# First weight unit behind the third load of x, later ones one load later; last weight loads every second step; ScalarE sends the last tile's first half

## The chip, the cores and the metric

One core of a Trainium2 chip. TensorE multiplies, VectorE, ScalarE and GpSimd work element by element, and SyncE (SP) issues most of the transfers. The metric is the device time of one execution in microseconds (us), the median of several timed executions.

## The reference

Two layers of gated products stand behind a Fourier transform of x along the sequence and along the features, of which the real part is kept:

```python
X = np.fft.fft(x, axis=1)              # x: (2, 3008, 256)
x = np.fft.fft(X, axis=2).real.reshape(6016, 256)
gate = 1 / (1 + np.exp(-(x @ w_gate))) # w_gate, w_val: (256, 1536)
x = gate * (x @ w_val) @ w_out         # w_out: (1536, 256)
h = x @ w_in                           # w_in: (256, 2048)
return (h * np.cos(h)) @ w_out2        # (2048, 256)
```

## The kernel before

The sequence transform of length 3008 is split into 47 times 64. The first part, of length 47, runs over 16 **chunks** of 8 feature pairs (L487); a **load of x** (`load_x2`) brings two chunks and is issued as three transfers of 32 partitions each (`rows`, L430). There are eight loads and three buffers, `raw` 0 to 2, so a load waits until TensorE has read the buffer's chunks of three loads earlier. PSUM holds three chunks; each is copied to SBUF (`evac`, L500 and L503) by VectorE or ScalarE. The first load comes in pieces of its own (L439, L440). Chunk 6 also needs a small extra tensor, `x0`. Then the second transform, of length 64 (L543, L544), and the third, over features (L583), follow.

Weights arrive as 64-bit patterns and are decoded on the chip in **units** of 512 KB by a chain of steps over ScalarE (L177, L152, L158, L190), VectorE (L153, L160, L164, L169) and GpSimd (L174, L238, L239, L193). `u_0_64` to `u_0_75` are the twelve units of the first layer's gate and value weights (`w1`), `u_0_76` to `u_0_80` and one more those of its output weights (`wo1`), and a small row unit (24 KB, in `eo_82` at first) comes ahead of all. The sixteen units of the second layer (`w2`) are decoded during the gating steps, written to DRAM (`ws`, L223) and read again later (`w2_load`, L715).

The 72 **gating steps** (`step1`) each take three-matmul products (L641 to L643), VectorE's L659 and L667, ScalarE's sigmoid (L853) and two casts, GpSimd's L671 and an accumulating transfer (L710), and four steps later the output products (L684 to L687). The last 192 steps make the second layer (L641 to L643 for the hidden values, L759 to L775 for the cosine, L739 for the output); each tile of results leaves by L743 and, for the last half, L753.

The order of instructions on each engine is written by a **planner** in the program itself: it keeps a clock for each engine (`clk`), gives each step of a unit a cost, and fills what it takes for idle time (`fill`, `slot`) up to a due time. The order is fixed when the program is built. At run time each engine works through its list and waits on semaphores. SP's queue is one such list: a transfer that has to wait holds back all that are listed behind it.

Of the kernel before, what the change touches and what calls it, by code (L numbers as in the profile page):

```python
# [40 lines left out]
L1, L2 = 4, 5  # L41
# [14 lines left out]
def fft_moe_moe(ctx: ExitStack, tc: tile.TileContext, x, x0, head, w1, w1s, wo1, w2, t1, t3, out):  # L56
# [9 lines left out]
    nc = tc.nc  # L66
    V, A, G, PE = nc.vector, nc.scalar, nc.gpsimd, nc.tensor
# [33 lines left out]
    def WO2(f):  # L101
        return slots[8 + f // 2][:, f % 2 * UC:(f % 2 + 1) * UC].rearrange("p (h m) -> p h m", h=2)
# [13 lines left out]
    sas = flat1[:, GV0 + 8 * TW:GV0 + 9 * TW].rearrange("p (g c) -> p g c", g=2)  # L116
# [9 lines left out]
    DQ = nc.sync  # L126
    clk = {V: 0.0, A: 0.0, G: 0.0, DQ: 0.0}
# [133 lines left out]
    def cost(step, e):  # L261
        return (step[1][e] if step[0] in (VG, VA) else step[1]) + (beside[0] if e is V else 0)

    def may(un, e):

        step = un[2][0]
        if step[0] not in (VG, VA):
            return e is step[0]
        if e not in step[0] or begun[0] and step[0] is VG and e is V:
            return False  # L270
        if begun[0] and step[0] is VG:
            return True
        other = step[0][1 - step[0].index(e)]
        mine, theirs = (max(un[3], clk[q]) + step[1][q] for q in (e, other))
        return mine <= theirs + (VLATE if e is V else 0)

    def room_at(at, forced=False):

        fits = [bf for bf in free if max(at, bf[2]) + LIFE <= bf[1] and (forced or bf[2] <= at + .3)]
        return min(fits, key=lambda bf: (bf[1], bf[2])) if fits else None  # L280

    def step_of(un, e=None):
        if len(un[2][0]) > 3 and not un[1]:
            at = max(un[3], clk[un[2][0][0]])
            while not (room_at(at, True) or free):
                finish(next(o for o in live if o[1] and o[0][0] in DIRECT))
            bf = room_at(at) or room_at(at, True) or free[0]
            free.remove(bf)
            un[1].append(bf)
            un[4].append(bf[0])  # L290
            un[3] = max(un[3], bf[2])
        step = un[2].pop(0)
        if step[0] in (VG, VA):
            e = e or (G if begun[0] and step[0] is VG else min(step[0], key=lambda q: max(clk[q], un[3]) + step[1][q]))
            step[2](e)
        else:
            e = step[0]
            step[2]()
        un[3] = spend(e, cost(step, e), un[3]) + ((5.0 if begun[0] else 3.3) if e is DQ else .15)
        if not un[2]:  # L300
            live.remove(un)
            free.extend([buf, end, un[3], of] for buf, end, _, of in un[1])

    def load_next():
        k = queued.pop(0)
        load(*k, slots[home(*k)])
        loaded[k] = spend(DQ, 1.5) + 2.8

    def pairs():

        found = [[bf for bf in free if bf[3] == of] for of in STAGES]
        return [pair for pair in found if len(pair) == 2]

    def start(bfs):
        for bf in bfs:
            free.remove(bf)
        k = todo.pop(0)
        room = [stages[STAGES.index(bfs[0][3])] if len(bfs) == 2 else bf[0] for bf in bfs[:1]]
        live.append([k, bfs, unit_steps(*k, room), max([loaded.get(k, 0.0)] + [bf[2] for bf in bfs]), room])

    def begin(until):

        while todo and todo[0] in loaded and loaded[todo[0]] <= until:
            start([])

    def fill(e, until):

        while True:
            begin(until)
            for un in live:  # L330
                step = un[2][0]
                if may(un, e):
                    at = max(un[3], clk[e])
                    if len(step) > 3 and not un[1] and not room_at(at):
                        continue
                    if at + cost(step, e) <= until:
                        step_of(un, e)
                        break
            else:
                if e is DQ and clk[e] + 1.5 <= until:  # L340
                    if queued:
                        load_next()
                        continue
                    if len(todo) > held[0] and todo[0][0] == "w2":
                        ready = [p for p in pairs() if max(bf[2] for bf in p) <= until]
                        if ready:
                            start(ready[0])
                            continue
                return
# [72 lines left out]
    with tc.tile_pool(name="xp", bufs=1) as xp:  # L422
# [9 lines left out]
        def load_x2(p):  # L432

            raw, src = raws[p % NX2].rearrange("p (c j) s n -> p c j s n", c=2), x[:, 2 * p:2 * p + 2]
            rows(DQ, raw, src)
            spend(DQ, 2.2)
# [19 lines left out]
        clk[DQ] = 4.3  # L456
        for p in range(1, NX2):
            load_x2(p)
            if p == 1:
                fill(DQ, clk[DQ] + 1.7)  # L460
        DQ.dma_start(out=xs[0:96], in_=x0)


        for _ in range(NWARM):
# [249 lines left out]
    def w2_load(u, q):  # L714
        q.dma_start(out=f32(slot_tile(u, F32R)), in_=ws[u])  # L715
# [5 lines left out]
    def hid(s):  # L721
        tt, f = divmod(s, NF2)
        y = ys[tt]
        o = ps[:, 4 + s % 4, 0:PC]
        for k in range(2):
            three(o, W2(f)[:, k, 0], W2(f)[:, k, 1], y[:, 0, k], y[:, 1, k], first=(k == 0), last=(k == 1))

    def out2(s):
        tt, f = divmod(s, NF2)
        h = h2.pop(s)  # L730
        last = s == N2S - 1


        order = [(0, 0, 0), (0, 1, 0), (1, 0, 0), (1, 1, 0), (0, 0, 1), (1, 0, 1)]
        if last:
            order = order[:2] + order[4:5]
        for d, i, m in order:
            o = ps[:, 2 * (tt % 2) + d, 0:PC]
            PE.matmul(o, WO2(f)[:, i, d * 128:(d + 1) * 128], h[:, m],  # L739
                      start=(f == 0 and i == m == 0), stop=(m == 1 and (f == NF2 - 1 or d == 1 and s == N2S - 2)))  # L740
            if m == 1 and f == NF2 - 1:
                A.mul(sas[:, d], o, 2.0)
                nc.sync.dma_start(out=out[tt, d], in_=sas[:, d])  # L743
            if m == d == 1 and s == N2S - 2:
                V.tensor_scalar(out=sas[:, 1], in0=o, scalar1=2.0, scalar2=None, op0=ALU.mult)
        if last:
            for k, c0 in enumerate((0, PC - 256)):
                o, new = ps[:, 4 + k, 0:256], slice(256 * k - c0 * k, 256)
                for i, m in ((0, 0), (1, 0), (0, 1)):
                    PE.matmul(o, WO2(f)[:, i, 128:], h[:, m, c0:c0 + 256], start=(i == m == 0), stop=(m == 1))  # L750
                y = sas[:, 1, 256 * k:256 + (PC - 256) * k]
                V.scalar_tensor_tensor(out=y, in0=o[:, new], scalar=2.0, in1=y, op0=ALU.mult, op1=ALU.add)
                nc.sync.dma_start(out=out[tt, 1, :, 256 * k:256 + (PC - 256) * k], in_=y)  # L753

    def cos_a(s):
        h = ps[:, 4 + s % 4, 0:PC]
        k = ks[s % 2].bitcast(I32)
        r = rt[s] = rs[s % 3]
        A.activation(out=k, in_=h, func=AF.Copy, scale=INV2PI)  # L759
        V.scalar_tensor_tensor(out=r, in0=k, scalar=-C1, in1=h, op0=ALU.mult, op1=ALU.add)  # L760
        V.scalar_tensor_tensor(out=r, in0=k, scalar=-C2, in1=r, op0=ALU.mult, op1=ALU.add)  # L761

    def cos_b(s):
        r = rt[s]
        A.activation(out=r, in_=r, func=AF.Abs)  # L765
        A.activation(out=r, in_=r, func=AF.Sin, scale=-1.0, bias=HALFPI)  # L766
        V.tensor_tensor(out=r, in0=r, in1=ps[:, 4 + s % 4, 0:PC], op=ALU.mult)  # L767

    def cos_c(s):
        r = rt.pop(s)  # L770
        if s % 2 == 0:
            pair[0] = ghs[s // 2 % 3]
        h = h2[s] = pair[0][:, s % 2]
        A.copy(h[:, 0], r)  # L774
        (V if s == N2S - 1 else G).tensor_tensor(out=h[:, 1], in0=r, in1=f32(h[:, 0]), op=ALU.subtract)  # L775
# [124 lines left out]
    late = list(range(NF1 - 1, 16))  # L900
    for s in range(L1, N2S + L2):
        if s < N2S:
            hid(s)
            cos_a(s)
        if s >= L2:
            out2(s - L2)
        if s - 1 < N2S:
            cos_b(s - 1)
        if s - 2 < N2S:
            cos_c(s - 2)  # L910
        if late:
            u = late.pop(0)
            need(("w2", u))
            w2_load(u, A)
        if s % NF2 == NF2 - 6 and s // NF2 + 1 < 2 * NPT:
            split_y(s // NF2 + 1)
# [91 lines left out]
```

## Time and profile before

| | |
|---|---|
| three timed runs | 1000.35, 999.75, 1000.3 us; median 1000.3 |
| profiled execution | 1000.49 us, its span 998.6 us |
| TensorE busy | 990.6 us (99%) |
| VectorE, ScalarE, GpSimd busy | 748.5 (75%), 787.2 (79%), 658.9 us (66%) |
| granted TensorE clock | 0.999 of full speed |
| chunks of the first transform | from 4.2 to 36.1 us |

The span is what the profile shows from the first to the last instruction; 1.9 us of the execution lie around it. TensorE's records are two per matmul of the transforms' 32-bit kind, and their ends are modelled. A wait is put down to whichever semaphore came last as far as the profile can tell, so an engine that it names may have been done long before.

### The profile page before, as it was taken

The numbers are of one execution on the slowest core, as the hardware profiler recorded it, in microseconds if no ns is written. First come the engines' busy times: TensorE is split into PE (matmuls) and PEld (weight loads), VectorE is DVE, ScalarE is ACT, GpSimd is POOL, SyncE is SP. The second block draws the span as 40 slices with busy tenths as digits, with TensorE's granted clock in tenths as the row PEclk, the third lists the DMA queues.
The fourth block names the chain that finished last, engine by engine and source line by source line (L and its number), as shares of the span: only waits on it lengthen the run. The fifth ranks groups of instructions, "written<-read, shape, count | busy, mean of one in ns | idle before, by whom it ended". The sixth has DMA issues, their size and how long they took to land.

```text
span 998.6 us, 13398 instructions
## 1 busy us (share of the span) xinstructions
PE 990.6 (99%) x4573; PEld 826.7 (83%) x4573; DVE 748.5 (75%) x1020; ACT 787.2 (79%) x1224; POOL 658.9 (66%) x528
## 2 busy tenths in 40 slices
PE   8999999999999999999999999999999999999998
PEld 8997888888888888888888888888888888888886
DVE  5888877788777778775768677776777777786775
ACT  4888666776776786776988888888888888888886
POOL 2778998988888888885546464554646455464543
PEclk9999999999999999999999999999999999999999
DMA  8804556677667667987300000000000000000000
GB/s 323 315 1 88 98 98 137 121 155 172 146 162 155 147 140 178 256 208 158 106 21 1 21 1 21 1 22 21 1 21 1 22 1 22 22 1 22 1 21 22
DMA packets 34788, 85.59 MB, mean 86 GB/s; under 512 B 3328, under 2 KB 25280, under 8 KB 34048
## 3 DMA queue, kind: packets, MB, share of 16 engines
q0 software_dynamic: 19584, 37.02, 21.6%
q1 hardware_dynamic: 14272, 45.07, 12.6%
q10 hardware_dynamic: 864, 2.66, 0.8%
q8 instruction: 36, 0.59, 0.2%
q14 instruction: 32, 0.26, 0.1%
HBM read 33.16 MB, written 14.56 MB: 48 GB/s over the span
## 4 chain that ended last, share of the span: by engine, by line
PE 97%; DMA 1%; DVE 1%; SPq 0%; ACT 0%; issue 0%
PE ps L739 26%; PE ps L641 15%; PE ps L643 15%; PE ps L642 15%; PE ps L684 7%; PE ps L687 7%; PE ps L686 7%; PE ps L487 2%; PE ps L583 2%; PE ps L543 1%; PE ps L544 1%; DMA u<-in_w_dram 1%; DMA early<-in_head_dram 0%; DVE D L667 0%; SPq L430 0%; DVE u L153 0%
## 5 line engine op out<-in xcount | busy, mean ns | idle before, releaser
L775 POOL TENSOR_TENSOR D<-D,D 128x502 fp32r<-128x502 f32 x191 | 249.4, 1306 | 252.6 <-ACT D L774 240.2
L739 PE MATMUL ps<-D,u 128*128 128x502 f32 x1149 | 291.2, 389 | 0.0
L643 PE MATMUL ps<-es,u 128*128 128x502 f32 x672 | 262.9, 391 | 0.0
L641 PE MATMUL ps<-es,u 128*128 128x502 f32 x672 | 262.5, 391 | 0.2 <-DVE D L667 0.2
L642 PE MATMUL ps<-es,u 128*128 128x502 f32 x672 | 262.0, 390 | 0.0
L739 PEld LDWEIGHTS ps<-D,u 128*128 128x128 f32 x1149 | 216.2, 188 | 45.3
L671 POOL TENSOR_TENSOR D<-D 128x502 f32<-128x502 f32 x144 | 197.6, 1508 | 40.9 <-ACT D L853 40.8
L760 DVE SCALAR_TENSOR_TENSOR D<-D,ps 128x502 f32<-128x502 int32 x192 | 130.2, 678 | 121.8 <-POOL D L775 102.1
L667 DVE TENSOR_TENSOR D<-D,ps 128x1004 f32<-128x1004 f32 x144 | 172.9, 1201 | 46.3 <-PE ps L643 28.2
L853 ACT ACTIVATE D<-D 128x1004 f32<-128x1004 f32 x72 | 75.1, 1043 | 106.6 <-DVE D L667 106.5
L759 ACT ACTIVATE D<-ps 128x502 int32<-128x502 f32 x192 | 113.3, 590 | 57.8 <-PE ps L643 55.2
L641 PEld LDWEIGHTS ps<-es,u 128*128 128x128 f32 x672 | 126.8, 189 | 27.5 <-DVE D L667 1.1
L642 PEld LDWEIGHTS ps<-es,u 128*128 128x128 f32 x672 | 127.0, 189 | 26.4
L643 PEld LDWEIGHTS ps<-es,u 128*128 128x128 f32 x672 | 126.5, 188 | 26.5
L761 DVE SCALAR_TENSOR_TENSOR D<-D 128x502 f32<-128x502 int32 x192 | 141.7, 738 | 6.6
L767 DVE TENSOR_TENSOR D<-D,ps 128x502 f32<-128x502 f32 x192 | 128.9, 671 | 15.2 <-ACT D L766 15.2
L659 DVE SCALAR_TENSOR_TENSOR D<-eo,w,ps 128x502 f32<-128x502 f32 x144 | 100.9, 733 | 32.4 <-PE ps L643 32.0
L766 ACT ACTIVATE D<-D 128x502 f32<-128x502 f32 x192 | 120.0, 625 | 6.1
L765 ACT ACTIVATE D<-D 128x502 f32<-128x502 f32 x192 | 118.7, 618 | 4.2 <-DVE D L761 2.8
L774 ACT CAST D<-D 128x502 fp32r<-128x502 f32 x192 | 114.5, 596 | 0.3 <-DVE D L767 0.3
L687 PE MATMUL ps<-D,u 128*128 128x502 f32 x288 | 112.2, 390 | 0.0
L686 PE MATMUL ps<-D,u 128*128 128x502 f32 x288 | 112.1, 389 | 0.0
(102 smaller groups left out, 1107.1 us busy)
## 6 DMA issues: line engine op xcount, KB each, us to landing
D<-D POOLq DMA_DIRECT2D x72, 502.0 KB, 5.5
D<-in_w_dram SPq DMA_DIRECT2D x16, 512.0 KB, 4.2
ws<-D SPq DMA_DIRECT2D x16, 512.0 KB, 4.5
u<-in_w_dram SPq DMA_DIRECT2D x12, 512.0 KB, 7.7
out_dram<-D SPq DMA_DIRECT2D x23, 251.0 KB, 2.5
u<-ws SPq DMA_DIRECT2D x11, 512.0 KB, 4.7
raw<-in_x_dram SPq DMA_DIRECT2D x21, 256.0 KB, 4.9
u<-in_wo_dram SPq DMA_DIRECT2D x6, 512.0 KB, 8.8
```

The costliest lines, as they stand in the source:

```text
L641: PE.matmul(o, w_hi, m_hi, start=first, stop=False)
L642: PE.matmul(o, w_lo, m_hi, start=False, stop=False)
L643: PE.matmul(o, w_hi, m_lo, start=False, stop=last)
L667: V.tensor_tensor(out=gv[s][:, :, c:c + PC], in0=sas, in1=ps[:, 6:8, 0:PC], op=op)
L671: G.tensor_tensor(out=gv[p][:, 1, m], in0=gv[p][:, 1, m], in1=gv[p][:, 0, m], op=ALU.mult)
L686: PE.matmul(o, WO1(f)[:, 0, m], h[:, 0, sg], start=first, stop=False)
L687: PE.matmul(o, WO1(f)[:, 1, m], h[:, 0, sg], start=False, stop=False)
L739: PE.matmul(o, WO2(f)[:, i, d * 128:(d + 1) * 128], h[:, m], start=(f == 0 and i == m == 0), stop=(m == 1 and (f == NF2 - 1 or d == 1 and ...
L760: V.scalar_tensor_tensor(out=r, in0=k, scalar=-C1, in1=h, op0=ALU.mult, op1=ALU.add)
L761: V.scalar_tensor_tensor(out=r, in0=k, scalar=-C2, in1=r, op0=ALU.mult, op1=ALU.add)
L767: V.tensor_tensor(out=r, in0=r, in1=ps[:, 4 + s % 4, 0:PC], op=ALU.mult)
L775: (V if s == N2S - 1 else G).tensor_tensor(out=h[:, 1], in0=r, in1=f32(h[:, 0]), op=ALU.subtract)
```

## The change

Ahead of the chunks, the first call of `fill` for SP's queue now stands behind the loads of x and not between the second and the third, and the planner's clock of that queue is moved on by 2.0 behind the transfer of `x0`. Since `fill` decides by that clock, all later weight loads shift in the list too. In the second layer the five last weight loads are issued at every second step. The first half of the last tile's result is issued from ScalarE's queue.

```diff
         for p in range(1, NX2):
             load_x2(p)
-            if p == 1:
-                fill(DQ, clk[DQ] + 1.7)
+        fill(DQ, clk[DQ] + 1.7)
         DQ.dma_start(out=xs[0:96], in_=x0)
+        clk[DQ] += 2.0
...
                 A.mul(sas[:, d], o, 2.0)
-                nc.sync.dma_start(out=out[tt, d], in_=sas[:, d])
+                (A if last else nc.sync).dma_start(out=out[tt, d], in_=sas[:, d])
...
-        if late:
+        if late and (s - L1) % 2 == 0:
             u = late.pop(0)
             need(("w2", u))
             w2_load(u, A)
```

SP's list, from the last part of the first load of x (`raw_115` is buffer 0, `raw_116` and `raw_117` are 1 and 2; `x3` are the three transfers of a load):

```order
 L440 DMA raw_115<-in_x_dram 96x1024
 L430 DMA raw_116<-in_x_dram 32x2048 x3
+L430 DMA raw_117<-in_x_dram 32x2048 x3
 L202 DMA eo_82<-in_w1s_dram 128x48
 L202 DMA u_0_64<-in_w_dram 128x1024
+L460 DMA early<-in_x_dram 96x256
+L430 DMA raw_115<-in_x_dram 32x2048 x3
+L202 DMA u_0_65<-in_w_dram 128x1024
+L430 DMA raw_116<-in_x_dram 32x2048 x3
+L202 DMA u_0_66<-in_w_dram 128x1024
 L430 DMA raw_117<-in_x_dram 32x2048 x3
-L461 DMA early<-in_x_dram 96x256
```

The third load of x, `raw_117`, moved ahead of the row unit and the first weight unit, and each later weight unit now follows the load of x that it stood ahead of. The sixth, `u_0_69`, moved behind the two tables that follow the last load.

ScalarE's list in the same stretch, from the first chunk's copy on, before:

```order
4 L503 COPY D_91<-ps 128x96x8 x2
5 L177 ACTIVATE eo_82<-eo_82 128x24
6 L177 ACTIVATE u_0_64<-u_0_64 128x512
7 L503 COPY D_91<-ps 128x96x8 x2
8 L177 ACTIVATE u_0_65<-u_0_65 128x512
9 L503 COPY D_91<-ps 128x96x8
10 L215 COPY w_88<-eo_82 128x24
```

and in the changed kernel:

```order
4 L503 COPY D_91<-ps 128x96x8 x3
5 L177 ACTIVATE eo_82<-eo_82 128x24
6 L152 ACTIVATE eo_82<-eo_82 128x24
7 L158 ACTIVATE eo_82<-eo_82 128x24
8 L503 COPY D_91<-ps 128x96x8
9 L177 ACTIVATE u_0_64<-u_0_64 128x512
10 L503 COPY D_91<-ps 128x96x8
11 L215 COPY w_88<-eo_82 128x24
```

The first decoding step of the row unit moved behind a third copy, and that of the first weight unit behind one more; the fourth chunk's copy went to VectorE.

GpSimd's list in the third to fifth gating step (L671 and L710 are the steps' own work, `es` belongs to the next tile's input), in the changed kernel:

```order
52 L671 TENSOR_TENSOR D_91<-D_91 128x502 x2
53 L710 DMA D_376<-D_91 128x2x502
54 L193 TENSOR_TENSOR es_679<-eo_83,es_679 128x502
55 L671 TENSOR_TENSOR D_91<-D_91 128x502 x2
56 L710 DMA D_376<-D_91 128x2x502
57 L174 TENSOR_TENSOR D_91<-D_91,u_0_79 128x512
58 L671 TENSOR_TENSOR D_91<-D_91 128x502 x2
59 L710 DMA D_376<-D_91 128x2x502
60 L193 TENSOR_TENSOR u_1_911<-D_91,u_1_911 128x2x256
```

Before, the L174 and the L193 of `u_0_79`, a unit of `wo1`, stood ahead of the first L671; they moved behind the fourth and fifth of L710's transfers.

## Rows read from the trace of the kernel before

**Rows 1.** The page's first line: span and instructions.

```profile
span 998.6 us, 13398 instructions
```

**Rows 2.** TensorE's waits: line, who released it, us, times, longest us.

```profile
PE ps L487 <- ACT D L503: 0.9, 1, 0.9
PE ps L487 <- DVE u L153: 0.7, 1, 0.7
PE ps L543 <- ACT D L508: 0.6, 1, 0.6
PE ps L487 <- DMA raw<-in_x_dram: 0.5, 1, 0.5
```

**Rows 3.** TensorE's timeline, first 90 us: start, us, records, idle before it.

```profile
6.66 5.60 PE L487 MATMUL ps<-early,raw 128*128 128x96 f32 x48 [0.45 <-DMA raw<-in_x_dram]
13.14 3.78 PE L487 MATMUL ps<-early,raw 128*128 128x96 f32 x32 [0.89 <-ACT D L503]
17.59 2.00 PE L487 MATMUL ps<-early,raw 128*128 128x96 f32 x16 [0.66 <-DVE u L153]
...
19.87 16.24 PE L487 MATMUL ps<-early,raw 128*128 128x96 f32 x144
...
84.25 0.49 PE L641 MATMUL ps<-es,u 128*128 128x502 f32 x1 [0.24 <-DVE D L667]
```

**Rows 4.** Timeline of SP's queue, 4 to 10 us: start and us of issue.

```profile
4.28 0.59 SPq L202 DMA_DIRECT2D eo<-in_w1s_dram  x1
6.58 0.35 SPq L202 DMA_DIRECT2D u<-in_w_dram  x1
7.03 1.75 SPq L430 DMA_DIRECT2D raw<-in_x_dram  x3
...
9.44 0.43 SPq L202 DMA_DIRECT2D u<-in_w_dram  x1
```

**Rows 5.** The same, last thirds of the third, fourth and eighth loads alone.

```profile
8.18 0.59 SPq L430 DMA_DIRECT2D raw<-in_x_dram  x1
...
11.13 0.59 SPq L430 DMA_DIRECT2D raw<-in_x_dram  x1
...
26.57 0.59 SPq L430 DMA_DIRECT2D raw<-in_x_dram  x1
```

**Rows 6.** These three in the view of transfers: size, us from issue to landing.

```profile
raw<-in_x_dram SPq DMA_DIRECT2D x1, 256.0 KB, 4.8
...
raw<-in_x_dram SPq DMA_DIRECT2D x1, 256.0 KB, 6.3
...
raw<-in_x_dram SPq DMA_DIRECT2D x1, 256.0 KB, 4.9
```

**Rows 7.** Busy time by stretch: PE, PEld, DVE, ACT, POOL, clock, DMA share, GB/s.

```profile
8.00:16.00 8.00, 7.12 (x65) 6.98 (x63) 2.05 (x5) 3.51 (x6) 0.23 (x1) 1.00 0.97 358
...
25.00:31.00 6.00, 6.00 (x56) 6.00 (x56) 5.36 (x8) 3.90 (x7) 4.90 (x5) 1.00 0.91 280
33.00:44.00 11.00, 10.43 (x93) 10.27 (x93) 9.29 (x18) 8.95 (x19) 8.12 (x10) 1.00 1.02 412
...
100.00:200.00 100.00, 100.00 (x440) 82.48 (x439) 79.50 (x89) 68.62 (x78) 94.76 (x81) 1.00 0.61 114
```

**Rows 8.** Timeline: a decoding step on GpSimd, an issue on ScalarE's queue.

```profile
73.09 1.30 POOL L193 TENSOR_TENSOR u<-D,u 128x512 fp32r<-128x512 f32 x1 [0.94 <-ACT u L190]
...
478.06 0.34 ACTq L715 DMA_DIRECT2D u<-ws  x1
```

**Rows 9.** Timeline of the end: VectorE's last pieces and SP's last issues.

```profile
994.08 0.77 DVE L752 SCALAR_TENSOR_TENSOR D<-ps,D 128x256 f32<-128x256 f32 x2 [0.35 <-PE ps L750]
994.34 0.33 SPq L743 DMA_DIRECT2D out_dram<-D  x1
994.77 0.88 SPq L753 DMA_DIRECT2D out_dram<-D  x2
```

**Rows 10.** The last transfer, by the page's list of issues.

```profile
out_dram<-D SPq DMA_DIRECT2D x1, 123.0 KB, 2.1
```

## Prediction

> **What bounds the kernel now.** I read the page first, then the list of what TensorE waited for, then TensorE's timeline, and only then the queue that feeds it. The page gives a span of 998.6 us [rows 1]. The list of waits is the reason why so small a change can show at all: over the whole span TensorE has a handful of waits, nearly all of them in the transforms [rows 2], the last of them at 84.25 [rows 3], and from there to the last matmul the view shows none. So whatever TensorE gains in the first 40 us is handed on to the end in full, as long as nothing later turns into a new wait; and time saved on any other engine is worth nothing by itself.
>
> The two waits that the change aims at are the 0.9 and the 0.7 us ahead of L487 [rows 2], the 96-column transform at the start. The view blames ScalarE's L503 and VectorE's L153. I don't believe it. The matmuls that start at 13.14 are chunk 4, which reads the third load of x, and those at 17.59 are chunk 6, which reads the fourth [rows 3]. The last third of the third load is issued at 8.18 and lands 4.8 us later, at 13.0; that of the fourth is issued at 11.13 and lands 6.3 us later, at 17.4 [rows 5, 6]. Both landings lie 0.1 to 0.2 us ahead of the matmul that waits. TensorE waits for x.
>
> How much is lost is better read from the pace than from the idle column, since ends of matmuls are modelled. The stretch from 19.87 runs 144 records, which are 9 chunks, in 16.24 us: 1.80 us a chunk [rows 3]. Three chunks from 6.66 would bring chunk 4 to 12.06; it starts at 13.14, 1.08 late. Two more bring chunk 6 to 16.74; it starts at 17.59, 0.85 late. Together **1.93 us**.
>
> **The change, part by part.** *Order of loads.* The queue's timeline shows what stands ahead of the third load (issued at 7.03): the 24 KB row unit at 4.28 and the 512 KB weight unit at 6.58 [rows 4]. Between the end of the first, 4.87, and 6.58 the queue issues nothing. After the change the third load comes first, so that its first third can fill that hole, and the 536 KB go behind it.
>
> What this is worth depends on the rate of the transfers. From 8 to 16 us it was 358 GB/s; the ends to choose from are 280 GB/s (25 to 31 us) and 412 GB/s (33 to 44 us) [rows 7], that is 350, 273 and 402 KB a us. I take the 350, since it is the stretch in question. 536 KB less ahead of the third load is 1.5 us (1.3 to 2.0): it lands at 11.5 or before, and chunk 4 wants it at 12.06. That wait goes, at any of the three rates.
>
> The fourth load has the row unit and the first weight unit ahead of it as before, but no longer the second weight unit, issued at 9.44 [rows 4]: 512 KB, 1.46 us. That alone brings 17.4 to 16.0. The hole that the first third of the third load fills (256 KB) is worth another 0.73, which brings it to 15.2. Chunk 6, with chunk 4 on time, wants it at 6.66 + 5 x 1.80 = 15.66. So the wait goes if the hole is really used, and 0.3 us of it stays if not. I take it as gone, since nothing but issue order kept the queue silent there.
>
> The later loads wait for a buffer that TensorE sets free, so they move with TensorE, and each has one weight unit less ahead of it than before. The tightest is the last: issued at 26.57 for its last third, landed 4.9 later at 31.5 [rows 5, 6], against chunk 14, which starts seven chunks after 19.87 [rows 3], at 32.5. That is 1.0 us of margin, and it should stay about that.
>
> The Trainium skill (DMA: Bandwidth & Descriptors, Where 436 GB/s comes from) speaks against so much room: it says that for HBM to SBUF the memory's side binds, at about 358 GB/s for a core. By that figure a pair of chunks would need 1,280 KB of x and weights in 3.66 us against a pace of 3.60, and the loads would fall behind by 0.06 us a pair, 0.3 us by the last: still inside the margin, so the sum would stay. The trace disagrees upward with its 412 GB/s and downward with its 280.
>
> Weight units arrive later for the sixth alone, which goes behind the two tables. Their decoding on ScalarE, VectorE and GpSimd stands in another order now (the pieces above); what a late unit costs is nothing until TensorE wants it. They are wanted in the gating steps only, whose one wait, at 84.25, is for L667 and not for a weight [rows 3], so a shift by one load, some 3.6 us, is covered by tens of them. The unit of wo1 that is decoded inside those steps now, and not ahead of them, adds its L174 and L193 (1.3 us each, by the L193 shown [rows 8]) to GpSimd there, whose busiest stretch is 100 to 200 us with 94.8 us busy of 100 [rows 7]: 5.2 us are free for some 2.6 more. Cost nothing; without that cover up to 2.6.
>
> *Late weight loads every second step.* The five issues on ScalarE's queue are 0.34 us each [rows 8], and TensorE has no wait anywhere near [rows 2, 3]. At most 5 x 0.34 = 1.7 us of ScalarE's time is spread out, behind TensorE. Worth 0; bounds 0 and 0, since a wait that isn't there can't be taken away, and the last unit comes 4 steps later with its use another 7 steps off.
>
> *ScalarE sends the last tile's first half.* At the end the queue issues L743 at 994.34 and the first L753 at 994.77, a slot of 0.43; the second L753 is half of 0.88 later, at about 995.2, while VectorE has its data ready at 994.08 + 0.77 = 994.85 [rows 9]. The last transfer lands 2.1 us after its issue [rows 10] and ends the program. With L743 off the queue the two can go at about 994.5 and 994.95. Gain 0.25; bounds 0 (the landing of the three overlaps anyway) and 0.43 (the whole slot).
>
> **Sum.** 1.93 + 0.25 = 2.2 us off the profiled execution: 1000.49 us with its span of 998.6, so 998.3 and 996.4. That execution is 0.2 above the median of the three timed runs, 1000.3; from the median I get **998.1**.
>
> **Rivals.** *A. Both waits go, and the tail with them* (the sum): 998.1, own range 997.7 to 998.7. Chance 0.58.
>
> *B. A smaller wait comes back in the transform.* The 0.3 us at chunk 6 if the hole isn't filled, or one at chunk 14 if the last load loses its 1.0 us of margin. For it: the rate falls to 280 GB/s in just the stretch where the last load travels [rows 7]. Against: that stretch has its 4.9 us in it already. With half of the 1.93 back and no tail gain, 999.2; the span is 998.7 to 999.7. Chance 0.24.
>
> *C. The head start is eaten later.* GpSimd, 95% busy [rows 7], takes the late unit badly, or VectorE's L667, which holds TensorE for 0.24 in the first gating steps [rows 3], does so longer. Up to 2.6 against 2.2: about 1000.3, no change. Against: a head start moves the work of all engines alike. Chance 0.08.
>
> *D. Slower: x itself becomes short.* If putting loads of x closer together drops the rate to the 280 GB/s of 25 to 31 us [rows 7] for the whole transform, a pair of chunks needs 1,280 / 273 = 4.69 us against 3.60, and four pairs lose 4.4: 1000.3 + 4.4 - 2.2 = 1002.5. It decides from 1,280 KB in 4.15 us a pair on (308 KB a us, 316 GB/s), where four losses of 0.55 eat the 2.2. Against: the 8 us at the start of the transform ran at 350, with loads of x and weights mixed. Chance 0.06.
>
> *E. More than the sum*: VectorE's order in the first steps also takes its 0.24 [rows 3], and ScalarE's 0.6 ahead of the second transform goes [rows 2]: 997.3. Chance 0.04.
>
> **How the numbers follow.** What a measurement of this kernel can tell from no change is about 0.2%, 2.0 us: the line is at 998.3, right beside the forecast. Of A 0.44 of its 0.58 lies below it, of E 0.04, of B 0.02: faster 0.50. D and a sliver of C make slower 0.07; the rest, 0.43, can't be told from no change. The range 997.6 to 999.6 leaves out most of C, all of D and the lower half of E, and a few hundredths of A and B: about 0.2.
>
> **What would show it.** Right: chunks 0 to 15 run in one stretch from 6.66 on, the second transform starts at about 34.8 (the chunks of rows 3 end at 36.1), the waits ahead of L487 but the first are gone, and the third load is issued in part before 6.6. Every later stage starts 1.9 us earlier with the wait of 0.6 at L543 as before. At the end ScalarE's issue stands where L743 stood, and the last landing follows the last matmul 0.25 sooner. Wrong: a wait ahead of L487 at chunk 6 or 14, a TensorE wait behind 90 us, or the last load landing more than 5.5 us after its issue.

## The result, and the profile after

The changed kernel takes **1006.14 us** (median of six runs, 1005.85 to 1006.67) against 1000.21 for the kernel before beside it: ratio 1.0058, 95% interval 1.0045 to 1.0071. It is slower by 5.9 us, where 2.2 less was forecast. The profiled execution is 1006.08 us, and its page begins:

```profile
span 1004.3 us, 13396 instructions
```

That is 5.7 more than in [rows 1]. The list of what TensorE waited for answers to [rows 2]:

```profile
PE ps L686 <- DVE D L169: 4.1, 1, 4.1
...
PE ps L543 <- ACT D L508: 0.6, 1, 0.6
PE ps L487 <- DMA raw<-in_x_dram: 0.4, 1, 0.4
PE ps L641 <- DVE D L667: 0.2, 1, 0.2
PE ps L686 <- ACT eo L698: 0.2, 1, 0.2
```

The two waits that the change aims at are gone. A new one of 4.1 us, of which there was no trace before, heads the list, and the last line is new too. TensorE's timeline shows where they lie (start, us, records, idle ahead):

```profile
6.66 11.24 PE L487 MATMUL ps<-early,raw 128*128 128x96 f32 x96 [0.45 <-DMA raw<-in_x_dram]
...
18.18 16.24 PE L487 MATMUL ps<-early,raw 128*128 128x96 f32 x144
34.99 0.49 PE L543 MATMUL ps<-early,D 128*128 128x128 f32 x2 [0.57 <-ACT D L508]
...
125.71 0.38 PE L643 MATMUL ps<-es,u 128*128 128x502 f32 x1
126.18 0.46 PE L686 MATMUL ps<-D,u 128*128 128x502 f32 x1
...
132.95 0.49 PE L686 MATMUL ps<-D,u 128*128 128x502 f32 x1 [0.17 <-ACT eo L698]
...
459.08 0.38 PE L643 MATMUL ps<-es,u 128*128 128x502 f32 x1
463.57 0.76 PE L686 MATMUL ps<-D,u 128*128 128x502 f32 x1 [4.11 <-DVE D L169]
464.12 0.62 PE L687 MATMUL ps<-D,u 128*128 128x502 f32 x1
464.54 0.62 PE L686 MATMUL ps<-D,u 128*128 128x502 f32 x1
...
467.05 1.68 PE L684 MATMUL ps<-D,u 128*128 128x502 f32 x4
468.56 0.39 PE L641 MATMUL ps<-es,u 128*128 128x502 f32 x1
```

The same place before the change, where the first products of the second layer (L641 to L643) and the last output products of the first (L684 to L687) take turns:

```profile
460.05 0.38 PE L643 MATMUL ps<-es,u 128*128 128x502 f32 x1
460.27 0.39 PE L686 MATMUL ps<-D,u 128*128 128x502 f32 x1
```

The balance, by start times of the same instruction in both traces:

| stretch | TensorE against before | what it is |
|---|---|---|
| chunks 0 to 15 | -1.69 | 34.99 against 36.68 [rows 3] |
| 126 and 133 us, and small steps to 459 | +0.72 | 459.08 against 460.05 is -0.97 |
| L643 to L686 | +4.27 | 4.49 from start to start, 0.22 before |
| the twelve products behind it | +2.25 | 463.57 to 468.56 is 4.99 us, 2.74 before |
| tail | +0.15 | the rest up to 5.7 |

The last but one row is TensorE's clock. Busy time by stretch (PE, PEld, DVE, ACT, POOL, clock, DMA share, GB/s):

```profile
450.00:460.00 10.00, 9.46 (x42) 7.51 (x40) 6.83 (x7) 7.75 (x10) 9.48 (x8) 1.00 0.81 160
460.00:465.00 5.00, 1.43 (x4) 1.21 (x5) 1.96 (x3) 1.33 (x2) 2.67 (x3) 0.65 0.77 195
465.00:468.00 3.00, 3.00 (x9) 2.39 (x8) 0.00 (x0) 0.66 (x1) 0.00 (x0) 0.50 0.34 60
468.00:475.00 7.00, 7.00 (x32) 5.77 (x31) 3.25 (x4) 5.19 (x8) 2.55 (x2) 0.98 0.43 73
```

TensorE had run without a gap since 133 us, then stood idle, and came back at a granted clock of 0.50, the lower of its two levels (1.2 GHz): a product every 0.42 us and not every 0.23, until 468.5. So the 4.3 us of waiting cost 6.5.

Why would TensorE wait for L169, a decoding step of a weight unit that it won't need for tens of us? VectorE's timeline, and ScalarE's:

```profile
455.49 2.43 DVE L667 TENSOR_TENSOR D<-D,ps 128x1004 f32<-128x1004 f32 x2 [0.70 <-PE ps L643]
461.43 0.68 DVE L760 SCALAR_TENSOR_TENSOR D<-D,ps 128x502 f32<-128x502 int32 x1 [3.51 <-ACT D L759]
462.14 0.68 DVE L761 SCALAR_TENSOR_TENSOR D<-D 128x502 f32<-128x502 int32 x1
462.74 0.68 DVE L169 SCALAR_TENSOR_TENSOR D<-D,ps 128x512 uint32<-128x512 uint32 x1
```

```profile
457.96 1.04 ACT L853 ACTIVATE D<-D 128x1004 f32<-128x1004 f32 x1 [2.06 <-DVE D L667]
458.90 1.01 ACT L782 CAST D<-D 128x1004 fp32r<-128x1004 f32 x1
459.83 1.03 ACT L783 ACTIVATE D<-D 128x1004 fp32r<-128x1004 f32 x1
460.77 0.57 ACT L759 ACTIVATE D<-ps 128x502 int32<-128x502 f32 x1
```

L169 ends at 463.42, and TensorE starts 0.15 later. Ahead of L169 stand L760 and L761, the first cosine steps of the second layer; they need L759, which stands on ScalarE behind the sigmoid L853, the cast L782 and L783. L169 stands behind them in VectorE's list and so runs after them, as the rows show. L169 reads a PSUM tile (`D<-D,ps`): three constants of the decoding lie in the last columns of **PSUM bank 0** from the sixth gating step on (`consts_in(0)`; sums of 502 columns leave 10 of 512 free), and bank 0 is what L686 writes first. The lists of the two built programs have the wait in plain sight. TensorE's first output product behind the first second-layer product, before and after (with the semaphores that it waits for), and VectorE's rows at the place:

```
1736 L686 MATMUL ps_63<-D2_383,u16_1_1301 128x502 [waits Activation_49]

1735 L686 MATMUL ps_63<-D2_376,u16_1_1300 128x502 [waits DVE_49,Activation_49]
...
409 L667 TENSOR_TENSOR D1_91<-D1_91,ps_63 128x2x502 [waits DVE_49]
410 L760 SCALAR_TENSOR_TENSOR D1_91<-D1_91,ps_63 128x502 [waits DMASW4_49,Activation_49,Pool_49]
411 L761 SCALAR_TENSOR_TENSOR D1_91<-D1_91 128x502 [waits DVE_49]
412 L169 SCALAR_TENSOR_TENSOR D1_91<-D1_91,ps_63 128x512 [waits PE_49]
```

The count of `DVE_49` that this L686 waits for is the one that the last L169 raises. Before the change the last L169 stood ahead of the last four gating steps, and so of any L760; it started at 437.6, 23 us before that L686. The Trainium skill (PSUM — Partial Sum Buffer, PSUM bank collisions raise a hardware error) says that two engines must be kept apart by semaphores for each bank (more exactly, each bank and 32 partitions), and not for each address. The built program does so, and the trace agrees: L169 reads a column that L686 never writes, and TensorE waits for its end.

### The profile page after: what moved, and what is told of

Its sections match the earlier page's. It is cut to its first block, busy times and chain, and to the rows that moved or that the text cites. A ratio compares the mean times of both kernels' runs of the same rounds, so it can differ in the third digit from the quotient of the medians.

```text
span 1004.3 us, 13396 instructions
## 1 busy us (share of the span) xinstructions
PE 993.3 (99%) x4573; PEld 828.0 (82%) x4573; DVE 747.1 (74%) x1015; ACT 792.7 (79%) x1229; POOL 657.9 (66%) x528
## 4 chain that ended last, share of the span: by engine, by line
PE 93%; POOL 3%; DVE 2%; ACT 1%; issue 1%; DMA 0%; SPq 0%; DVEq 0%; POOLq 0%; ACTq 0%
PE ps L739 26%; PE ps L643 14%; PE ps L641 14%; PE ps L642 14%; PE ps L686 6%; PE ps L684 6%; PE ps L687 6%; PE ps L487 3%; PE ps L583 1%; PE ps L543 1%; PE ps L544 1%; POOL D L671 1%; DVE D L667 1%; POOL D L710 1%; DMA raw<-in_x_dram 0%
## 5 line engine op out<-in xcount | busy, mean ns | idle before, releaser
L643 PE MATMUL ps<-es,u 128*128 128x502 f32 x672 | 262.9, 391 | 0.0
L641 PE MATMUL ps<-es,u 128*128 128x502 f32 x672 | 262.5, 391 | 0.3 <-DVE D L667 0.2
L671 POOL TENSOR_TENSOR D<-D 128x502 f32<-128x502 f32 x144 | 198.2, 1520 | 44.7 <-ACT D L853 44.6
L760 DVE SCALAR_TENSOR_TENSOR D<-D,ps 128x502 f32<-128x502 int32 x192 | 130.2, 678 | 127.4 <-POOL D L775 101.8
L667 DVE TENSOR_TENSOR D<-D,ps 128x1004 f32<-128x1004 f32 x144 | 172.9, 1201 | 47.4 <-PE ps L643 23.3
L759 ACT ACTIVATE D<-ps 128x502 int32<-128x502 f32 x192 | 113.1, 589 | 58.4 <-PE ps L643 55.7
L853 ACT ACTIVATE D<-D 128x1004 f32<-128x1004 f32 x72 | 75.1, 1044 | 96.0 <-DVE D L667 95.8
L641 PEld LDWEIGHTS ps<-es,u 128*128 128x128 f32 x672 | 126.8, 189 | 27.5 <-DVE D L667 1.1
L761 DVE SCALAR_TENSOR_TENSOR D<-D 128x502 f32<-128x502 int32 x192 | 143.9, 750 | 6.6
L643 PEld LDWEIGHTS ps<-es,u 128*128 128x128 f32 x672 | 126.4, 188 | 26.5
L659 DVE SCALAR_TENSOR_TENSOR D<-eo,w,ps 128x502 f32<-128x502 f32 x144 | 101.2, 735 | 32.8 <-PE ps L643 32.3
L686 PE MATMUL ps<-D,u 128*128 128x502 f32 x288 | 113.3, 393 | 4.4 <-DVE D L169 4.1
L687 PE MATMUL ps<-D,u 128*128 128x502 f32 x288 | 113.1, 393 | 0.0
```

What stands on the lines that cost most here:

```text
L641: PE.matmul(o, w_hi, m_hi, start=first, stop=False)
L643: PE.matmul(o, w_hi, m_lo, start=False, stop=last)
L667: V.tensor_tensor(out=gv[s][:, :, c:c + PC], in0=sas, in1=ps[:, 6:8, 0:PC], op=op)
L671: G.tensor_tensor(out=gv[p][:, 1, m], in0=gv[p][:, 1, m], in1=gv[p][:, 0, m], op=ALU.mult)
L686: PE.matmul(o, WO1(f)[:, 0, m], h[:, 0, sg], start=first, stop=False)
L687: PE.matmul(o, WO1(f)[:, 1, m], h[:, 0, sg], start=False, stop=False)
```

## Experiments

Two theories. **Bank**: the wait is this chain, L643, L759, L760, L761, L169, L686, and only the shared bank closes it. **Late unit**: the last unit of the second layer, decoded later, makes data late (GpSimd's L671 and L710, ScalarE's casts), and L169 is just the name that the view gives.

**1. Constants in another bank** (of the changed kernel).

```diff
-                consts_in(0)
+                consts_in(3)
```

> The changed kernel, but the constants lie in PSUM bank 3, which the same four lines of products reach six matmuls later. Theory (bank): the first six products run on time and the seventh waits, so the wait moves from the first L686 to the seventh product and shrinks by 6 x 0.2275 = 1.4 us, from 4.3 to 2.9. Time 1004.7 if the clock falls as before, 1002.6 if a wait of 2.9 us leaves the clock alone. Rival (late unit): the wait stays at the first L686 with 4.1 us, 1006.1.

1004.28 us, ratio to the kernel before 1.0038 (1.0026 to 1.0050). The wait moved to the seventh product and shrank to 2.7:

```profile
463.63 0.49 PE L686 MATMUL ps<-D,u 128*128 128x502 f32 x1 [2.67 <-DVE D L169]
463.96 0.39 PE L687 MATMUL ps<-D,u 128*128 128x502 f32 x1
```

The bank decides which instruction waits, as the first theory says to within 0.2. In this profile the clock stayed at 1.00; of the five runs two had a mean of 1.0 (1002.8, 1003.2 us) and three 0.998 (1004.3 to 1005.2).

**2. Constants in SBUF** (of the changed kernel): they move to `kc`, a small SBUF tile.

```diff
-                consts_in(0)
+                cs = [kc[:, c:c + 1] for c in (1, 2, 0)]
...
+    kc = cpool.tile([128, 4], F32, name="kc")
```

> The changed kernel, but the three decoding constants of the gating steps (read by L153, L160, L164 and L169) lie in SBUF and not in columns 509 to 511 of PSUM bank 0, the bank that L686 and L687 write. Order of instructions unchanged. Theory (bank): TensorE's wait of 4.1 us at 463.57 is for VectorE's last L169, only because that reads bank 0; it goes, and the stretch at half clock behind it with it: 4.3 + 2.2 = 6.5 off 1006.1, so 999.6. Rival (late unit): the last second-layer unit makes the data of the output product late (GpSimd's L671 and L710, ScalarE's casts), and L169 is only the name that the view gives: no change, 1006.1.

1047.0 us, ratio 1.0466 (1.0450 to 1.0482). The wait for L169 is gone from TensorE's list, but the forecast of 999.6 failed by 47 us, through something that neither theory had:

```profile
PE ps L641 <- DVE D L659: 15.7, 8, 3.9
PE ps L641 <- DVE D L667: 11.0, 10, 1.7
```

Two of VectorE's decoding steps, L164 and L169, became long (out<-in, xcount, busy, mean ns):

```profile
L169 DVE SCALAR_TENSOR_TENSOR D<-D,kc 128x512 uint32<-128x512 uint32 x23 | 35.9, 1562 | 0.5
L164 DVE SCALAR_TENSOR_TENSOR D<-D,kc 128x512 f32<-128x512 f32 x16 | 33.4, 2090 | 0.1
```

against 686 and 681 ns with the constant in PSUM. So this run can't tell what the wait at the transition alone is worth. The next rows, VectorE's longest L169 and GpSimd's work at that time, show the reason:

```profile
161.65 7.35 DVE L169 SCALAR_TENSOR_TENSOR D<-D,kc 128x512 uint32<-128x512 uint32 x1
...
161.79 1.71 POOL L193 TENSOR_TENSOR u<-D,u 128x512 fp32r<-128x512 f32 x1
163.04 2.91 POOL L671 TENSOR_TENSOR D<-D 128x502 f32<-128x502 f32 x2
165.48 1.64 POOL L710 DMA_DIRECT2D D<-D  x1
166.26 2.18 POOL L174 TENSOR_TENSOR D<-D,u 128x512 int32<-128x512 int32 x1
```

Each L164 and L169 with `kc` that no GpSimd operation overlaps takes 0.68 to 0.69 us; the long ones (1.1 to 7.35) lie beside GpSimd's operations for most of their time, those above 4 us for nine tenths of it or more. With both inputs in SBUF these VectorE steps are held up while GpSimd works, though not always: three that it overlaps for 0.57 or 0.58 us took no longer than alone. The Trainium skill (SBUF — State Buffer, SBUF: two separate sides) names the lock: a port pair that the two share, which a VectorE operation with two SBUF inputs needs while GpSimd reads SBUF. These rows agree, and show besides that several GpSimd operations in a row can go ahead of one VectorE step. In this kernel PSUM is the better place for the constants.

**3. ScalarE's first cosine step ahead of the casts** (of the changed kernel), alone and with bank 3.

```diff
-        if 2 <= s <= N1S + 1:
+        if 2 <= s <= N1S + 1 and main:
             hi_at = hi1(s - 2)
...
             cos_a(i)
+        if N1S <= s <= N1S + 1:
+            hi_at = hi1(s - 2)
```

> The changed kernel with ScalarE's L759 of the first two second-layer steps put ahead of the casts L782 and L783 that it stood behind. Theory (chain L643, L759, L760, L761, L169, L686): L759 can start when the first hidden product is done, at 459.5 and not at 460.77, so TensorE's wait shrinks by 1.3, from 4.3 to 3.0. Time 1004.8 where the clock still falls behind it, 1002.6 where not. Rival (late unit): the wait is for something else than this chain and stays at 4.1 or grows, since the casts come later: 1006.1 or more.

1005.82 us, ratio 1.0053 (1.0040 to 1.0066). The wait is 3.4, so it follows the chain, but by 0.7 and not by 1.3: L759 now starts 0.50 after ScalarE's last L853, where it has to wait for the products, and L761 takes 1.24 and not 0.68 us beside GpSimd's L671 (both its inputs lie in SBUF, as in 2). All five runs show a mean clock of 0.998. The profiled one also waits 0.69 for x ahead of chunk 6.

> The edit of the last kernel and the constants in PSUM bank 3 together. Theory: both shorten the same wait, 4.3 - 1.3 - 1.4 = 1.6 or less, ahead of the seventh product. The clock: a wait of 2.7 us let it fall in three of five runs; if a shorter one leaves it alone, all runs show 1.0 and the time is 1001.2 (1000.6 to 1001.8); if any wait does it, 1003.4. Rival (late unit): over 1004.

1004.33 us, ratio 1.0035 (1.0023 to 1.0048). The wait is 2.0, by both steps together, and stands at the seventh product. The time is above both expected ones, 1001.2 and 1003.4, and by itself it would fall to the rival (over 1004). The trace decides for the chain: it has the wait in the forecast place, a wait of 0.69 for x ahead of chunk 6 that belongs to neither theory, and the slow clock again. The mean clock is 0.997 or 0.998 in three of the five runs, of which the profiled one is one. By stretch:

```profile
455.00:461.00 6.00, 6.00 (x28) 4.99 (x27) 3.27 (x4) 3.78 (x6) 6.00 (x6) 1.00 0.70 120
461.00:464.00 3.00, 1.05 (x5) 0.59 (x4) 2.49 (x3) 1.86 (x3) 2.08 (x3) 0.95 0.79 234
464.00:467.00 3.00, 3.00 (x8) 2.39 (x8) 0.00 (x0) 0.00 (x0) 0.61 (x1) 0.50 0.67 121
467.00:472.00 5.00, 5.00 (x23) 4.11 (x23) 1.36 (x2) 3.71 (x5) 0.74 (x1) 0.99 0.19 33
```

**4. Which edit does it?** The first edit alone; the two others alone; and the first edit's two halves, the added line and the moved call.

> The kernel before with the change's first edit alone (order of the loads, and the planner's clock of SP's queue moved on by 2.0). Theory: this edit alone moves the last second-layer unit's L169 behind the first L760 and L761, so the wait is there in full: 1005.9 to 1006.1, span 1004.1 or so. Rival (late loads): the last weight loads at every second step have a part in the wait at the transition: then clearly below 1006, near 999.5.

1007.07 us, ratio 1.0072 (1.0059 to 1.0085), with the wait of 4.1. Its runs go from 1005.7 to 1010.3, and in the profiled one the clock fell a second time, in the first transform (0.73 from 18 to 24 us), behind a wait of 1.5 for the fourth load of x.

> The kernel before with the second and third edits alone (last weight loads at every second step, ScalarE sends the last first half). Theory: no new wait, and the tail behind the last matmul is longer by 0.16 as in the profile of the changed kernel (3.94 against 3.78 from the start of the last L750 to the last landing): 1000.4. Rival (the prediction's term): the tail is 0.25 shorter, 999.95. Rival (late loads hurt): a TensorE wait appears in the second layer, over 1001.

1000.29 us, ratio 0.9999 (0.9991 to 1.0008): no new wait, and no change that can be told. So the first edit carries the loss.

```diff
         DQ.dma_start(out=xs[0:96], in_=x0)
+        clk[DQ] += 2.0
```

> The kernel before with one added line, the 2.0 on the planner's clock of SP's queue; the loads of x keep their old order. Theory: that number alone shifts the second layer's units so far that the last L169 falls behind the first L760: the wait of 4.1 and the half clock behind it appear without any other edit, 1000.2 + 6.5 = 1006.7 (1005.8 to 1007). Rival (it takes the loads' new order as well): 1000.2.

1006.82 us, ratio 1.0063 (1.0050 to 1.0075): the 2.0 alone, a number that changes no load of x, brings the wait of 4.1 in full.

```diff
             load_x2(p)
-            if p == 1:
-                fill(DQ, clk[DQ] + 1.7)
+        fill(DQ, clk[DQ] + 1.7)
```

> The kernel before with the first call of fill moved behind the loads, without the 2.0 on the planner's clock. In VectorE's list the last unit's L164 and L169 then stand behind the second L760 and L761. Theory (L169 holds the next write to PSUM bank 0): TensorE waits at the second output product of the transition for L169, about 3.5 us by the rows of VectorE, and the clock falls behind it (2.0): 1005 (1004 to 1006.5). Rival (only the 2.0 does harm, or the wait is for the unit itself): 999 to 1000.3.

1008.28 us, ratio 1.0083 (1.0069 to 1.0096), above the expected 1004 to 1006.5. The wait is 4.6, not 3.5, for an L169 that now stands behind two cosine steps, with the clock at 0.71 behind it. The rest of the loss, which was not expected, is in the first transform: three waits for loads of x, 3.4 us in all.

**5. Second looks at both kernels.**

> The kernel before, a second profile. How much do its two waits of the first transform vary? By the prediction they are the load order's own (1.08 and 0.85): both there again within 0.2, second transform's start at 36.7. If they are partly chance: another sum, by half a us or more.

> The changed kernel, a second profile. The wait of 4.1 at the transition and the half clock behind it again within 0.1. In the first transform: no wait at chunks 4 and 6 if the new order covers them, one of 0.7 to 1.5 at chunk 6 if its margin is as thin as three of the last profiles with this order show.

The kernel before took 999.86 us here, and only one of its two waits came back:

```profile
6.87 5.60 PE L487 MATMUL ps<-early,raw 128*128 128x96 f32 x48 [0.40 <-DMA raw<-in_x_dram]
13.32 5.57 PE L487 MATMUL ps<-early,raw 128*128 128x96 f32 x48 [0.85 <-ACT D L503]
```

Its second transform starts at 35.98 and not at 36.68; the two other profiles with the old order (late_send, clk_only) have it at 35.9. The changed kernel took 1006.73 us; the wait is 4.1 again, and the second transform starts at 34.95. The slow clock behind the wait lasted longer than expected, and cost 2.85 by start times and not 2.25. Of the other seven profiles with its order of loads four have that start at 35.1 or 35.2, and three, with a wait of 0.7 to 1.5 ahead of chunk 6, at 35.8, 36.0 and 37.5.

**6. Mending it.** First, the second layer's units one gating step earlier:

```diff
-    PSTART, PACE, NW2 = 18, 16 / 47, 16
+    PSTART, PACE, NW2 = 17, 16 / 47, 16
```

> The changed kernel with one number of the planner changed: the second layer's units may start one gating step earlier (PSTART 17 and not 18), so that the last unit's L169 stands ahead of the first L760 in VectorE's list, as before the change. Theory (L169 behind L760 is the cause): no wait at the transition and no fall of the clock, 1006.1 - 4.3 - 2.2 = 999.6, and below that by what the two small waits at 126 and 133 us (0.6) happen to do: 999.0 to 999.8. Rival (the later load order or the 2.0 on the planner's clock hurt in another way): still over 1002.

1000.02 us, ratio 0.9997 (0.9988 to 1.0006), just above the expected 999.0 to 999.8. With L169 ahead of L760 again the wait and the slow clock are gone, 6.1 us below the changed kernel by one number. The small waits at 126 and 133 are still there (0.56 by start times). Then also those, and SP as the sender:

```diff
-                (A if last else nc.sync).dma_start(out=out[tt, d], in_=sas[:, d])
+                nc.sync.dma_start(out=out[tt, d], in_=sas[:, d])
...
-            if not (s > L1 and ends(s - L1 - 1)):
+            if not (s > L1 and (ends(s - L1 - 1) or s == L1 + BLK - 1)):
                 ahead(V, now + 3 * MM)
```

> The changed kernel with PSTART 17, with VectorE's decoding steps kept out of the one gating step in which the first tile's product ends (there L153, L160 and L164 stood in a row ahead of L659), and with the last first half sent by SP as before. Theory: no wait at the transition, the two small waits at 126 and 133 us (0.6 together) gone, the tail as before: what is left of the loads' order alone, 0.5 to 1.7 us below the kernel before, 998.7 to 999.9. Rival (the small waits come from the later weight unit on GpSimd, not from VectorE's three steps): they stay, and the time is that of the last fix, 1000.0.

999.53 us, ratio 0.9992 (0.9983 to 1.0001): the best of all, by 0.9 us, though the interval just touches no change. All of TensorE's waits in its profile:

```profile
PE ps L465 <- POOL early L441: 1.0, 1, 1.0
PE ps L543 <- ACT D L508: 0.6, 1, 0.6
PE ps L641 <- DVE D L667: 0.2, 1, 0.2
```

The waits at 126 and 133 are gone with VectorE's three steps in a row, so those were their cause, not GpSimd, whose rows from 118 to 128 us are the same as with PSTART 17 alone.

## Why the prediction was wrong

**The step that failed** is the one on the weight units: "what a late unit costs is nothing until TensorE wants it". It followed the first units into the gating steps, where their data has tens of us to spare, and stopped. It also had the units arrive later "for the sixth alone", while SP's list, shown with the change, has each one behind one more load of x, and in the trace the first four are issued 1.7 to 2.4 later (the first at 8.35 and not 6.58 [rows 4]). Two things were missed. A shift by one unit runs through the planner's whole list and comes out at its other end: the last unit's L169 slid from the gating steps to behind the first L760. And an engine can wait for a decoding step without wanting its result: the step reads the bank that TensorE writes next. The wait costs 4.27 and the clock behind it 2.25 (2.85 in the second look), against a forecast of 0. What the forecast had named as its sign of failure, a TensorE wait behind 90 us, is what the trace shows. This term alone makes the loss: without it (the mend by PSTART) the time is 1000.0, though that still lies above the range of 997.6 to 999.6, by the terms that follow.

**Waits of the first transform: mechanism right, size too large.** In the profiled pair the two waits went and TensorE gained 1.69 of 1.93. That TensorE waited for x there, and not for the engines that the view named, is borne out by late_send and clk_only, where the view names `raw<-in_x_dram` for the wait of 1.1 and 1.0 ahead of chunk 4. The 1.93 was one execution's, though: three other profiles with the old order have one of the two waits and start the second transform 0.7 to 0.8 sooner, so that the new order is worth some 0.8 us (35.9 against 35.1) where no load comes late, and some 0.6 in the mean of the four profiles with the old order (36.1) against the nine with the new (35.5). Its margin at chunk 6 is thinner than worked out, too. The fourth load's last third is issued at 10.51 and lands 5.1 later, at 15.6, where 15.2 was forecast; chunk 6 starts at 15.90, and in three of nine profiles with this order the load comes later than that. The hole in SP's queue was used in part: the third load's first third goes out at 4.34, the next at 6.57. So the queue is silent from 4.9 to 6.6 with either order, and the forecast's "nothing but issue order kept the queue silent there" is wrong; what did stays open. Rival B, a smaller wait come back, was real, and stands beside the main case and not against it.

**Decoding inside the gating steps (rival C): place wrong, size small.** GpSimd took the late unit without harm. VectorE did not: three of its steps now stand in a row ahead of L659,

```profile
123.16 1.32 DVE L153 SCALAR_TENSOR_TENSOR u<-u,ps 128x512 uint16<-128x512 uint16 x1
124.51 0.69 DVE L160 SCALAR_TENSOR_TENSOR u<-u,ps 128x512 uint32<-128x512 uint32 x1
125.35 0.69 DVE L164 SCALAR_TENSOR_TENSOR D<-u,ps 128x512 f32<-128x512 f32 x1
125.95 1.38 DVE L659 SCALAR_TENSOR_TENSOR D<-eo,w,ps 128x502 f32<-128x502 f32 x2
```

where two stood before (L659 at 126.83), so VectorE, and ScalarE's L698 behind it, is 0.9 early where TensorE is 1.7 early. That is most of the +0.72. The forecast's reason against C, "a head start moves the work of all engines alike", doesn't hold here. At 126 the wait is the main one in small: L164 reads bank 0 and ends at 126.04, and L686 starts at 126.18. With the constants in bank 3 it is gone there, but VectorE's three steps still stand in a row, and TensorE waits for L667 at 130.18 instead.

**Late loads at every second step: 0**, as forecast: late_send, which has this edit and the next, shows no new wait (1000.29 against 1000.22).

**ScalarE sends the first half: -0.25 forecast, +0.15 found** in the traces; the timed runs of late_send can't tell it from 0. The issues moved as worked out: the last two leave SP from 1000.09, 0.45 behind the start of VectorE's first L752 at 999.64, and before it was 0.69 [rows 9]. But the last transfer took longer to land:

```profile
out_dram<-D ACTq DMA_DIRECT2D x1, 251.0 KB, 2.5
out_dram<-D SPq DMA_DIRECT2D x1, 128.0 KB, 2.5
out_dram<-D SPq DMA_DIRECT2D x1, 123.0 KB, 2.5
```

2.5 us against 2.1 [rows 10]; it is 2.5 again in late_send, 2.8 with PSTART 17, and 2.2 in the mended kernel, where SP sends. The three transfers travel together, and what leaves earlier lands no earlier. The forecast had this as its lower bound, 0, and chose the middle; what was found lies outside.

**Rival D (x short of bandwidth)** gave the right side for the wrong reason. It shows only in part, as chance: order_noclk's three waits and the one of 1.5 in the first edit alone.

## What to carry to other kernels

Where a planner writes the order, a change at the front of its list has to be followed to the list's end: compare the two built lists engine by engine at every change of stage, with the semaphores that each instruction waits for, and look for an instruction of the bottleneck engine that has gained one. Whatever lies in a PSUM bank that accumulates, here a constant of one column, ties each reader's place in its engine's list to TensorE's next write there. And a wait that one trace shows is worth its size in that execution: a second look at the kernel before would have halved the largest term here.

## What the runs showed of the hardware

- A wait of TensorE has a second price, the time at half clock behind it (2.25 and 2.85 us in two executions of the changed kernel). The mean clock is 0.998 or less in every run of the kernels whose wait is 3.4 us or more, and in three of five both where it is 2.7 and where it is 2.0; the kernel before shows 0.999 or 1.0.
- VectorE's decoding steps L164 and L169 over 512 columns took 0.68 us alone and up to 7.35 beside GpSimd with both inputs in SBUF; with one input in PSUM they take 0.67 to 0.69 throughout the changed kernel.
- The first matmuls behind the warm-up start 0.21 us apart (by records) for up to 2.4 us in some executions (pstart17: 4.52 to 6.87) and 0.11 apart in others (the changed kernel's first profile): 10 records against 17 from 4.30 to 6.00, with a granted clock of 1.00 for that stretch in both. What decides it stays open.
